# Moving one PSUM copy per pair to ScalarE, and the loads of the gate's weights and of w_out, in an attention and two-MoE kernel

## The chip, the core and the metric

The kernel runs on one core of a Trainium2 chip. A core has five engines, each with an instruction queue of its own that runs in order: TensorE (PE, matmuls, writes to PSUM only), VectorE (DVE), ScalarE (ACT), GpSimd (POOL) and SyncE (SP, which here issues nearly all DMAs). SBUF is the working memory, PSUM takes matmul results, DRAM lies behind 16 DMA engines. The metric is the device time of one execution in microseconds, lower is better.

## The reference

Three layers, on 4 batches of 448 tokens with 12 heads of 64 (1792 tokens, width 768):

```
attention:  q_n, k_n = rmsnorm(q)*g_q, rmsnorm(k)*g_k
            x = softmax(q_n @ k_n.T / sqrt(64)) @ v            # 48 (batch, head) pairs of 448 x 448
MoE 1:      h = x @ w_in            # 768 -> 2048
            g = where(h > 0, h, exp(min(h, 0)) - 1)            # ELU
            y = g @ w_out           # 2048 -> 768
MoE 2:      logits = y @ w_gate     # 768 -> 8 experts
            route tokens greedily by sorted logits, 224 per expert
            out[token] = relu(y @ w1[e]) @ w2[e]               # 768 -> 1024 -> 768
```

`w_in` and `w_out` arrive as 64-bit floats, the rest as 32-bit floats. To keep enough precision with 16-bit matmuls, most operands are split into a high and a low fp16 half, and a product is three matmuls (high x high, low x high, high x low).

## The kernel before

The first part runs attention for all batches and, one batch behind it, the hidden layer of MoE 1. The unit of attention is a *pair* of heads (`Pair`, 24 of them, numbered 0 to 23); two pairs share a `Duo`, which loads q, k and v, normalises q and k and turns them. A pair has 448 query rows, in three blocks of 128 (j = 0, 1, 2) and a tail of 64 (j = 3). For each block:

- `scores`: six matmuls for two heads A and B into two PSUM tiles `ps`, VectorE takes each row's maximum (L533), ScalarE the exponential with its row sum (L535);
- `weights`: VectorE takes reciprocals (L540, L541), GpSimd scales the rows (L545);
- `turn_p`: TensorE transposes A's weights, with a corner of B's, into the PSUM tile `ta` and B's into `tb`; ScalarE copies `ta` (128x512) to `PT` in SBUF (L559) and VectorE copies `tb` (128x384, L560).

After the tail, `values` multiplies with v into `po`, and ScalarE and VectorE evict it, split in halves, to `xT` (L578, L579). The PSUM tiles `ta`, `tb`, `po`, `pw` (gate products) and `pl` (logits) share the three buffers of one pool, `psT`.

`hidden(b)` multiplies `xT` of batch b with `w_in`: 16 blocks f of 18 matmuls each into `ph`, then ELU on ScalarE and VectorE (L682 to L688), and stores the result `gt` to DRAM (`g_d`, `gt_d`).

The second matrix of MoE 1 and the gate are joined ahead of time: the logits are g @ (w_out @ w_gate). So `gate_products` goes through `w_out` in 16 blocks of 128 rows. `load_steps` loads 64-bit numbers by SP into one of three buffers `st`, VectorE assembles 32-bit floats from their bits with three integer instructions per part (L374, L377, L378; a block has a part of 512 and one of 256 columns), ScalarE scales and casts (L380, L381), GpSimd subtracts to get the low half (L382). The block `wo` is stored to `wo_d` for later use (L610) and turned by two transposing DMAs (L614); `gate_product` multiplies the turned block with the gate's weights `wg16` and leaves 8 columns in `Wg` through one ScalarE and four VectorE instructions (L627 to L631). `load_gate` loads the gate's weights (L598) and splits them on ScalarE and VectorE (L599, L600). `w_in` is loaded by the same `load_steps`.

`logits` adds up four blocks of g against `Wg` into `acc` (L647, L649). For batches 2 and 3 that happens inside `hidden`; for batches 0 and 1 `late_logits` loads g back from DRAM (`gl`, L658, L659).

The order of the work is planned in steps t from -48 to 387: a pair has 16 steps, pair n starts its scores at step 16n and its `values` come at 16n+19. `at(t, f)` puts a function at a step, `Spread(gen, n, t0, t1)` spreads n steps of a generator evenly over t0 to t1, `hidden(b)` runs over the 96 steps that begin with 96(b+1)+5. From the order in which instructions are written a scheduler makes each engine's queue; it may put an instruction ahead of others written earlier if its inputs and its buffer are free. Two kinds of instruction are tied to the plan: the first integer instruction of each part of `w_in` or `w_out` (L374) can't come ahead of the last score maximum written before it, and a hidden block's first matmuls not ahead of scores written shortly before them.

After step 387 the hidden layer of batch 3, the second matrix of MoE 1, the routing and the experts follow. Their code isn't touched.

Of the kernel before, what the change touches and what calls it, by code (L numbers as in the profile page):

```python
# [8 lines left out]
F16 = mybir.dt.float16  # L9
# [246 lines left out]
def kernel(  # L256
# [14 lines left out]
    nc = tc.nc  # L271
    PE, ACT, DVE, POOL = nc.tensor, nc.scalar, nc.vector, nc.gpsimd

    B, H, S, D = q.shape
# [5 lines left out]
    P = 128  # L280
    NP = H // 2
    KC = DM // P
    NF = FF // P
    NF1 = F1 // P
    DH = DM // 2
    NJ = 3
    MAIN = NJ * P
    TAIL = S - MAIN
# [33 lines left out]
    def mm(o, l, r, key=None, **kw):  # L322

        i = PE_mm(o, l, r, **kw)  # L324
        if key is not None:
            if key in last_in_bank:
                tc.add_manual_dep(i.ins, last_in_bank[key].name, NOSYNC, reason="order in a bank")
            last_in_bank[key] = i.ins
        return i
# [6 lines left out]
    g_d = [dram.tile([P, NF, 2, MAIN], F16, name=f"g_d{b}") for b in range(B)]  # L336

    gt_d = [dram.tile([P, NF, 2, 2 * TAIL], F16, name=f"gt_d{b}") for b in range(B // 2)]
# [18 lines left out]
    def load_steps(hi, lo, src):  # L357

        w = src.shape[1]
        if src.dtype == F32:  # L360
            st = stg.tile([P, w], F32, tag="st", name="st")
            i = nc.sync.dma_start(st, src)
            if hold:
                tc.add_manual_dep(i.ins, hold[-1].ins.name, NOSYNC, reason="not before its turn")
            split(hi, lo, st, w)
            yield
            return

        for a in range(0, w, 512):
            n = min(512, w - a)  # L370
            st = stg.tile([P, n, 2], I32, tag="st", name="st")
            nc.sync.dma_start(st.rearrange("p n t -> p (n t)"), src[:, a:a + n].bitcast(I32))
            cv = gat.tile([P, n], I32, tag="cv", bufs=3, name="cv")
            i = DVE.tensor_scalar(cv, st[:, :, 1], 3, 0x3FFFFFF8, op0=ALU.logical_shift_left, op1=ALU.bitwise_and)  # L374
            if pace:
                tc.add_manual_dep(i.ins, pace[-1].ins.name, NOSYNC, reason="not before its turn")
            DVE.scalar_tensor_tensor(cv, st[:, :, 1], -0x40000000, cv, op0=ALU.bitwise_and, op1=ALU.bitwise_or)  # L377
            DVE.scalar_tensor_tensor(cv, st[:, :, 0], 29, cv, op0=ALU.logical_shift_right, op1=ALU.bitwise_or)  # L378
            cf = cv.bitcast(F32)
            ACT.activation(cf, cf, AF.Copy, scale=SW)  # L380
            ACT.copy(hi[:, a:a + n], cf)  # L381
            POOL.tensor_sub(lo[:, a:a + n], cf, hi[:, a:a + n])  # L382
            yield
# [13 lines left out]
    def key():  # L397
        n_key[0] += 1
        return n_key[0]
# [4 lines left out]
    gat = att_s.enter_context(tc.tile_pool(name="gat", bufs=2))  # L404
# [3 lines left out]
    psT = ps1.enter_context(tc.tile_pool(name="psT", bufs=3, space=PSUM))  # L408
# [89 lines left out]
    class Pair:  # L498
# [48 lines left out]
        def turn_p(s, j):  # L547

            p = s.P.pop(j)[0].rearrange("p u k -> p (u k)")
            ta = psT.tile([P, NJ + 1, P], F32, tag="pt", name="pta")  # L550
            for c in range(NJ):
                mm(ta[:, c, :], p[:, c * P:(c + 1) * P], id32, is_transpose=True, start=True, stop=True)
            mm(ta[:, NJ, :], p[:, MAIN:MAIN + 2 * TAIL], id32, is_transpose=True, start=True, stop=True)
            if j < NJ:
                tb = psT.tile([P, NJ + 1, P], F32, tag="pt", name="ptb")
                for c in range(NJ):
                    mm(tb[:, c, :], p[:, S + TAIL + c * P:S + TAIL + (c + 1) * P], id32, is_transpose=True, start=True, stop=True)
                cs = slice(j * P, (j + 1) * P)
                ACT.copy(s.PT[:, 0:NJ + 1, cs], ta)  # L559
                DVE.tensor_copy(s.PT[:, NJ + 1:, cs], tb[:, 0:NJ])  # L560
            else:
                ACT.copy(s.PT[:, 0:NJ, MAIN:S], ta[:, 0:NJ, 0:TAIL])
                ACT.copy(s.PT[0:TAIL, NJ, MAIN:S], ta[0:TAIL, NJ, 0:TAIL])
                DVE.tensor_copy(s.PT[:, NJ + 1:, MAIN:S], ta[:, 0:NJ, TAIL:])
                DVE.tensor_copy(s.PT[TAIL:, NJ, MAIN:S], ta[TAIL:, NJ, TAIL:])
# [31 lines left out]
    def load_gate():  # L597
        nc.sync.dma_start(wg32, w_gate.rearrange("(c p) e -> p c e", p=P))  # L598
        ACT.activation(wg16[:, :, 0:NE], wg32, AF.Copy, scale=-SW)  # L599
        DVE.scalar_tensor_tensor(wg16[:, :, NE:], wg32, -SW, wg16[:, :, 0:NE], op0=ALU.mult, op1=ALU.subtract)  # L600

    def gate_products():
        wts = None
        for f in range(NF):
            wo = gat.tile([P, 2, DM], F16, name="wo")
            yield from load_steps(wo[:, 0, :], wo[:, 1, :], w_out[f * P:(f + 1) * P, :])
            if f:
                gate_product(f - 1, wts)
                yield
            nc.sync.dma_start(wo_d[:, f], wo)  # L610
            wts = []
            for z in range(2):
                wts.append(gat.tile([P, KC, P], F16, name="wt", bufs=3))
                nc.sync.dma_start_transpose(wts[z], wo[:, z, :])  # L614
            yield
        gate_product(NF - 1, wts)
        yield

    def gate_product(f, wts):
        pw = psT.tile([P, 2 * NE], F32, tag="pt", name="pw")  # L620
        for z in range(2):
            n = NE if z else 2 * NE
            for c in range(KC):
                mm(pw[:, 0:n], wts[z][:, c, :], wg16[:, c, 0:n], start=(z == 0 and c == 0),
                   stop=(z == 1 and c == KC - 1), skip_group_check=True)
        t = gat.tile([P, NE], F32, name="wgt")
        ACT.copy(t, pw[:, NE:])  # L627
        DVE.tensor_add(t, t, pw[:, 0:NE])
        DVE.tensor_copy(Wg[:, f, 0:NE], t)
        DVE.tensor_copy(Wg[:, f, WG:], t)  # L630
        DVE.tensor_sub(Wg[:, f, NE:2 * NE], t, Wg[:, f, 0:NE])  # L631

    LG = 4

    def logits(pool, tag, b, gs):

        pl = pool.tile([P, S], F32, tag=tag, name="pl")
        kk = key()
        for i, (g, f) in enumerate(gs):
            for z, (o, n) in enumerate(((0, WG), (WG, NE))):  # L640
                mm(pl[o:o + n], Wg[:, f, o:o + n], g[:, z, :], key=kk,
                   start=(i == 0), stop=(i == len(gs) - 1), skip_group_check=True)
        n = WG + NE
        for o, w, c in ((b * MAIN, MAIN, 0), (B * MAIN + b * TAIL, TAIL, MAIN)):
            a = acc[:, o:o + w]
            if gs[0][1] == 0:
                DVE.tensor_copy(a, pl[0:n, c:c + w])  # L647
            else:
                DVE.tensor_add(a, a, pl[0:n, c:c + w])  # L649

    LB = 2

    def late_logits(b):
        for f in range(0, NF, LG):
            gs = []
            for i in range(f, f + LG):
                gl = gat.tile([P, 2, S], F16, bufs=LG, name="gl")
                nc.sync.dma_start(gl[:, :, 0:MAIN], g_d[b][:, i])  # L658
                nc.sync.dma_start(gl[:, :, MAIN:S], gt_d[b // 2][:, i, :, b % 2 * TAIL:(b % 2 + 1) * TAIL])  # L659
                gs.append((gl, i))  # L660
            yield
            logits(psT, "pt", b, gs)
            yield

    def hidden(b, xT):

# [28 lines left out]
        if b >= LB:  # L695
            logits(psT, "pt", b, gs[NF - LG:NF])
# [14 lines left out]
    def chain_gens(gens):  # L711
        for g in gens:
            yield from g

    def w_in_steps(u):
        for c in range(KC):
            load_w_in(u, c)
            yield
# [5 lines left out]
    def at(t, f, *a):  # L724
        todo.setdefault(t, []).append((f, a))

    NG = NF * (2 + DM // 512 + 1)
    spreads = [
        Spread(w_in_steps(0), KC, 40, 96),
        Spread(chain_gens(w_in_steps(i) for i in range(1, FF // WB)), KC * (FF // WB - 1), 96, 176),  # L730
        Spread(gate_products(), NG, 180, 280),
        Spread(chain_gens(late_logits(b) for b in range(LB)), 2 * LB * NF // LG, 295, 400),
    ]
    at(-47, load_gain)
    at(-30, load_gate)
    NSTEP = B * SEQ
    for b in range(B):
        xT = big.tile([P, KC, 2, S], F16, name="xT")
# [122 lines left out]
    for o in range(0, NCH, h):  # L861
        pt = psR.tile([P, h, n], F32, tag=f"rt_pb{4 if o else 0}", name="plt")
# [152 lines left out]
```

## Time and profile before

| what | value |
|---|---|
| median of three runs | 1150.81 us (1146.79 to 1153.8) |
| the profiled execution | 1149.89 us |
| its span, first to last instruction | 1148.2 us |
| mean granted TensorE clock | 0.968 of full speed |
| busy: PE, DVE, ACT, POOL | 1037.0, 787.0, 538.5, 354.1 us |

Busy time is the union of an engine's instructions; matmuls are pipelined and their ends are modelled, so a busy TensorE isn't one at its peak. An instruction that waits inside an engine for a shared resource counts as busy too. The DMA share is the mean busy share of the 16 DMA engines.

### The profile page before, as it was taken

The page shows a single profiled execution, that of the slowest core. Times are in us where ns is not written, and L with a number is a line of the kernel's source. Part 1 is how long each engine was busy: PE and PEld are TensorE (multiplying, and loading weights), DVE is VectorE, ACT ScalarE, POOL GpSimd, SP SyncE. Part 2 cuts the span into 40 slices and gives each one's busy share as a digit, 9 for nine tenths or more (in the row PEclk, how much of TensorE's full clock was granted, in tenths as well). Part 3 has the DMA queues.
Part 4 walks back from the last instruction along what each step waited for, and adds up shares of the span by engine and source line. Part 5 has one row for each costly group of instructions (what it writes and reads, how often), then busy time and mean ns, then how long its engine had stood idle before and what let it go on. Part 6 is the DMA issues. An engine that isn't in the chain of part 4 may idle for free.

```text
span 1148.2 us, 19348 instructions
## 1 busy us (share of the span) xinstructions
PE 1037.0 (90%) x7030; PEld 608.9 (53%) x7030; DVE 787.0 (69%) x1567; ACT 538.5 (47%) x1099; POOL 354.1 (31%) x462
## 2 busy tenths in 40 slices
PE   0687879897989989999999999999999799999997
PEld 0233434443544444444444545555546688888885
DVE  3798898999988775654334778887786556666620
ACT  2676677776867765554441111011112455555510
POOL 3677686657756542221001000000000412222100
PEclk9977889999999999999999999999999899999999
DMA  6355575559998736334922151131133778777710
GB/s 173 80 123 130 136 206 164 152 162 246 259 246 207 193 74 135 97 80 148 398 78 69 59 196 59 49 132 49 49 104 100 238 244 247 255 252 255 239 41 25
DMA packets 190319, 176.48 MB, mean 154 GB/s; under 512 B 114704, under 2 KB 161808, under 8 KB 189456
## 3 DMA queue, kind: packets, MB, share of 16 engines
q1 hardware_dynamic: 186064, 163.78, 49.7%
q0 software_dynamic: 3328, 11.01, 3.0%
q8 instruction: 55, 0.90, 0.3%
q10 hardware_dynamic: 832, 0.46, 0.1%
q14 instruction: 40, 0.33, 0.1%
HBM read 125.92 MB, written 31.98 MB: 138 GB/s over the span
## 4 chain that ended last, share of the span: by engine, by line
PE 51%; DVE 18%; DMA 11%; issue 10%; ACT 5%; POOL 3%; SPq 2%; POOLq 0%; DVEq 0%; ACTq 0%
PE py L324 18%; PE ph L324 11%; DMA st<-in_moe_w_dram 4%; PE pye L324 4%; PE po L324 4%; PE phe L324 3%; DVE sm L533 2%; PE ps L324 2%; PE rt_pc L324 2%; DVE cv L377 2%; PE pta L324 2%; DMA qn<-in_q_dram 2%; PE pl L324 1%; DVE cv L378 1%; DVE rt_C L127 1%
## 5 line engine op out<-in xcount | busy, mean ns | idle before, releaser
L324 PE MATMUL ph<-xT,w_in 128*128 128x448 f16 x1152 | 247.2, 359 | 7.8 <-DVE elu_g L685 4.8
L324 PE MATMUL py<-w_out,g 128*128 128x384 f16 x1152 | 203.8, 328 | 0.0
L324 PEld LDWEIGHTS <-w_in 128*128 128x128 f16 x1152 | 108.0, 99 | 125.4 <-issue 44.7
L545 POOL TENSOR_SCALAR pe<-pe,sm 128x448 f32<-128x448 f32 x168 | 127.0, 766 | 141.0 <-DVE sm L541 78.9
L351 DVE SCALAR_TENSOR_TENSOR w<-st,w 128x768 f16<-128x768 f32 (+1 forms) x112 | 119.4, 1073 | 72.1 <-ACT w L350 65.8
L324 PEld LDWEIGHTS <-g 128*128 128x128 f16 x1152 | 107.3, 98 | 81.4 <-issue 18.5
L350 ACT ACTIVATE w<-st 128x768 f16<-128x768 f32 (+1 forms) x112 | 103.8, 933 | 89.3 <-DMA st<-in_moe_w_dram 84.0
L324 PE MATMUL ps<-kT,qT 64*128 64x448 f16 (+1 forms) x576 | 94.3, 382 | 54.5 <-ACT pe L535 29.2
L535 ACT ACTIVATE pe<-ps,sm 128x448 f32<-128x448 f32 x168 | 105.7, 633 | 50.1 <-DVE sm L533 47.6
L324 PE MATMUL pye<-w,hT 128*112 128x512 f16 (+1 forms) x768 | 126.4, 326 | 0.0
L127 DVE TENSOR_SCALAR rt_C<-rt_row,rt_m 128x1792 f16<-128x1792 f32 x98 | 107.3, 1149 | 8.2 <-PE rt_pc L324 7.4
L533 DVE TENSOR_REDUCE sm<-ps 128x1 f32<-128x448 f32 x168 | 100.2, 614 | 17.8 <-PE ps L324 15.5
L324 PEld LDWEIGHTS <-w 128*128 128x128 f16 x1152 | 110.4, 99 | 3.3 <-DVE xTe L922 1.2
L324 PE MATMUL phe<-xTe,w 128*128 128x224 f16 x1080 | 109.2, 261 | 2.1 <-DVE xTe L922 1.1
L324 PEld LDWEIGHTS <-hT 128*112 128x112 f16 x768 | 91.6, 130 | 32.1
L815 ACT ACTIVATE xh<-py 128x384 f16<-128x384 f32 x28 | 13.7, 490 | 176.6 <-PE py L324 159.2
L324 PEld LDWEIGHTS <-qT 64*128 64x128 f16 (+1 forms) x576 | 27.5, 100 | 99.0 <-issue 65.9
L324 PE MATMUL pta<-id,pe 128*128 128x128 f32 x384 | 65.3, 293 | 12.7 <-POOL pe L545 4.7
L685 DVE SCALAR_TENSOR_TENSOR elu_g<-ph,elu_e 128x448 f32<-128x448 f32 x64 | 39.6, 618 | 48.0 <-ACT elu_e L683 47.7
L972 POOL DMA_INDIRECT out_dram<-yo,idx x16 | 18.5, 1155 | 173.9 <-DVE yo L971 172.3
L324 PEld LDWEIGHTS pta<-id,pe 128*128 128x128 f32 x384 | 46.1, 148 | 43.1 <-POOL pe L545 16.0
L201 POOL MEMSET rt_c<- 128x8 f16 x8 | 0.9, 123 | 210.1 <-DVE rt_c L207 206.0
(176 smaller groups left out, 1475.1 us busy)
## 6 DMA issues: line engine op xcount, KB each, us to landing
st<-in_moe_w_dram SPq DMA_DIRECT2D x48, 512.0 KB
st<-in_moe_w_dram SPq DMA_DIRECT2D x64, 384.0 KB
st<-in_moe_w_in_dram SPq DMA_DIRECT2D x24, 512.0 KB
g_d<-gt SPq DMA_DIRECT2D x64, 192.0 KB
g<-g_d SPq DMA_DIRECT2D x16, 768.0 KB
st<-in_moe_w_out_dram SPq DMA_DIRECT2D x16, 512.0 KB
gl<-g_d SPq DMA_DIRECT2D x32, 192.0 KB
wo_d<-wo SPq DMA_DIRECT2D x16, 384.0 KB
```

The source lines that it names most:

```text
L127: i = DVE.tensor_scalar(C.rearrange("p c t -> p (c t)"), row, m[:, s:s + 1], None, op0=ALU.is_le)
L324: i = PE_mm(o, l, r, **kw)
L350: ACT.activation(hi, st, AF.Copy, scale=SW)
L351: DVE.scalar_tensor_tensor(lo, st, SW, hi, op0=ALU.mult, op1=ALU.subtract)
L377: DVE.scalar_tensor_tensor(cv, st[:, :, 1], -0x40000000, cv, op0=ALU.bitwise_and, op1=ALU.bitwise_or)
L378: DVE.scalar_tensor_tensor(cv, st[:, :, 0], 29, cv, op0=ALU.logical_shift_right, op1=ALU.bitwise_or)
L533: i = DVE.tensor_reduce(out=st[:, 0, u:u + 1], in_=ps[u], axis=AX.X, op=ALU.max, negate=True)
L535: ACT.activation(p[:, u, :], ps[u], AF.Exp, bias=st[:, 0, u:u + 1], accum_out=st[:, 1, u:u + 1])
L545: POOL.tensor_scalar(p[:, u, :], p[:, u, :], st[:, 2, u:u + 1], 1.0, op0=ALU.mult, op1=ALU.mult)
L685: DVE.scalar_tensor_tensor(gf, ph, -SG / SH, e, op0=ALU.mult, op1=ALU.min)
L815: ACT.activation(xh[:, 0], py, AF.Copy, scale=-SX2 / (SG * SW))
L972: st = POOL.indirect_dma_start(out=out, out_offset=bass.IndirectOffsetOnAxis(ap=idx[:, 1, 2 * e + hh:2 * e + hh + 1], axis=0), in_=yo, in_ ...
```

## The change

Four edits:

- for the middle block of each pair (j = 1) `tb` is copied to `PT` by ScalarE, no longer by VectorE;
- `gate_products` is spread over steps 240 to 368, before over 180 to 280;
- `late_logits` takes the two batches in turn for each group of four blocks, before one batch after the other, and is spread over steps 285 to 400, before 295 to 400;
- `load_gate` is put at step 100, before at -30.

The list `ready` is only bookkeeping while the program is built: it makes sure that logits are written after the gate products that they read.

```diff
@@ Pair.turn_p
                 ACT.copy(s.PT[:, 0:NJ + 1, cs], ta)
-                DVE.tensor_copy(s.PT[:, NJ + 1:, cs], tb[:, 0:NJ])
+                (ACT.copy if j == 1 else DVE.tensor_copy)(s.PT[:, NJ + 1:, cs], tb[:, 0:NJ])
@@ gate_products
+    ready = []
+
     def gate_products():
-        wts = None
         for f in range(NF):
...
             if f:
                 gate_product(f - 1, wts)
+                ready.append(f - 1)
                 yield
...
         gate_product(NF - 1, wts)
+        ready.append(NF - 1)
         yield
@@ logits
+        assert gs[-1][1] in ready
@@ late_logits
-    def late_logits(b):
+    def late_logits():
         for f in range(0, NF, LG):
-            gs = []
-            for i in range(f, f + LG):
-                gl = gat.tile([P, 2, S], F16, bufs=LG, name="gl")
-                nc.sync.dma_start(gl[:, :, 0:MAIN], g_d[b][:, i])
-                nc.sync.dma_start(gl[:, :, MAIN:S], gt_d[b // 2][:, i, :, b % 2 * TAIL:(b % 2 + 1) * TAIL])
-                gs.append((gl, i))
-            yield
-            logits(psT, "pt", b, gs)
-            yield
+            for b in range(LB):
+                gs = []
+                for i in range(f, f + LG):
+                    gl = gat.tile([P, 2, S], F16, bufs=LG, name="gl")
+                    nc.sync.dma_start(gl[:, :, 0:MAIN], g_d[b][:, i])
+                    nc.sync.dma_start(gl[:, :, MAIN:S], gt_d[b // 2][:, i, :, b % 2 * TAIL:(b % 2 + 1) * TAIL])
+                    gs.append((gl, i))
+                yield
+                logits(psT, "pt", b, gs)
+                yield
@@ the plan
-        Spread(gate_products(), NG, 180, 280),
-        Spread(chain_gens(late_logits(b) for b in range(LB)), 2 * LB * NF // LG, 295, 400),
+        Spread(gate_products(), NG, 240, 368),
+        Spread(late_logits(), 2 * LB * NF // LG, 285, 400),
...
-    at(-30, load_gate)
+    at(100, load_gate)
```

## Rows read from the trace of the kernel before

**Rows 1.** The page: busy us (share of the span) xinstructions, and the chain.

```profile
PE 1037.0 (90%) x7030; PEld 608.9 (53%) x7030; DVE 787.0 (69%) x1567; ACT 538.5 (47%) x1099; POOL 354.1 (31%) x462
...
PE 51%; DVE 18%; DMA 11%; issue 10%; ACT 5%; POOL 3%; SPq 2%; POOLq 0%; DVEq 0%; ACTq 0%
```

**Rows 2.** Timeline of ScalarE: start us, us, engine, line, operation, out<-in.

```profile
254.67 0.53 ACT L578 ACTIVATE xT<-po 128x448 f16<-128x448 f32 x1
```

**Rows 3.** Stretches: from:to, us, busy us (x) of each engine, clock, DMA share, GB/s.

```profile
core 0: us, PE busy (x) PEld busy (x) DVE busy (x) ACT busy (x) POOL busy (x), PEclk, DMA share, GB/s
55.71:254.67 198.96, 171.53 (x893) 78.93 (x894) 178.63 (x341) 143.47 (x333) 136.35 (x164) 0.89 0.58 149
169.28:190.06 20.78, 20.78 (x124) 10.55 (x124) 16.46 (x30) 14.83 (x35) 11.86 (x14) 1.00 0.56 153
235.89:254.67 18.78, 18.78 (x108) 8.65 (x107) 16.29 (x39) 15.17 (x38) 8.46 (x12) 1.00 0.55 155
254.67:280.48 25.81, 21.77 (x145) 10.59 (x144) 25.70 (x55) 18.01 (x45) 19.96 (x24) 1.00 1.03 251
280.48:303.92 23.44, 18.61 (x130) 10.12 (x130) 22.78 (x58) 16.05 (x42) 16.50 (x16) 0.85 0.99 253
303.92:330.27 26.35, 24.46 (x156) 12.00 (x156) 25.73 (x59) 21.72 (x55) 17.65 (x24) 1.00 0.97 247
...
407.19:421.56 14.37, 10.10 (x71) 5.26 (x71) 12.50 (x30) 9.37 (x28) 8.41 (x13) 1.00 0.08 17
254.67:359.69 105.02, 92.10 (x601) 45.64 (x600) 99.32 (x229) 75.12 (x185) 69.57 (x82) 0.95 0.99 251
359.69:521.06 161.37, 151.66 (x970) 74.89 (x969) 107.97 (x269) 99.61 (x245) 59.86 (x87) 1.00 0.51 120
521.06:538.59 17.53, 17.53 (x106) 8.99 (x108) 8.15 (x19) 8.33 (x19) 2.21 (x4) 1.00 0.36 90
```

**Rows 4.** Stretches, instructions on `ph` alone: us, then PE, DVE, ACT busy.

```profile
169.28:190.06 20.78, 12.53 (x60) 1.23 (x2) 1.09 (x2) 1.00 0.56 153
235.89:254.67 18.78, 9.31 (x42) 1.24 (x2) 1.62 (x3) 1.00 0.55 155
...
407.19:421.56 14.37, 1.46 (x6) 0.00 (x0) 0.00 (x0) 1.00 0.08 17
```

**Rows 5.** A stretch, instructions on `cv` alone: us, then DVE, ACT, POOL busy.

```profile
218.00:410.00 192.00, 58.59 (x104) 35.37 (x70) 38.40 (x37) 0.96 0.82 208
```

**Rows 6.** A stretch, instructions on `wgt` alone: us, then DVE, ACT busy.

```profile
254.67:420.00 165.33, 18.10 (x64) 2.57 (x16) 0.97 0.86 214
```

**Rows 7.** Timeline of VectorE: one unit of logits, of nine up to 521 us.

```profile
461.14 0.66 DVE L649 TENSOR_TENSOR acc<-acc,pl 40x384 f32<-40x384 f32 x2
```

**Rows 8.** Groups by line and shape: xcount | busy us, mean ns | idle before.

```profile
L559 ACT COPY PT<-pta 128x512 f32<-128x512 f32 x72 | 41.8, 583 | 9.7 <-PE pta L324 9.5
...
L560 DVE COPY PT<-ptb 128x384 f32<-128x384 f32 x72 | 39.4, 547 | 4.8 <-PE ptb L324 4.7
...
L377 DVE SCALAR_TENSOR_TENSOR cv<-st,cv 128x512 int32<-128x512 int32 x40 | 36.7, 916 | 0.0
...
L562 ACT COPY PT<-pta 128x192 f32<-128x192 f32 x24 | 7.6, 318 | 5.0 <-PE pta L324 5.0
```

**Rows 9.** Line L377: duration ns min/median/max, first and last start us, forms.

```profile
L377 DVE SCALAR_TENSOR_TENSOR cv<-st,cv x56: 411/681/2171, 66.6 to 389.1; 128x512 int32<-128x512 int32 x40, 128x256 int32<-128x256 int32 x16
```

**Rows 10.** Timeline of the first microseconds: SP, ScalarE and VectorE around the gate's weights.

```profile
11.36 1.54 SPq L372 DMA_DIRECT2D st<-in_moe_w_in_dram  x3
...
11.77 0.24 ACT L599 ACTIVATE wg<-wg 128x48 f16<-128x48 f32 x1 [3.03 <-DMA wg<-in_moe_w_gate_dram]
...
11.92 0.95 ACT L451 ACTIVATE sq<-kn 128x896 f32<-128x896 f32 x1
12.04 1.99 DVE L600 SCALAR_TENSOR_TENSOR wg<-wg,wg 128x48 f16<-128x48 f32 x1 [0.38 <-ACT wg L599]
13.96 1.07 DVE L452 TENSOR_REDUCE ss<-sq 128x14 f32<-128x896 f32 x1
```

## The prediction

> **What bounds the kernel now.** I read the busy shares and the chain of waits first, then the span cut into stretches at the ends of the attention pairs, then the groups by line, then the first 30 us. Over the whole span TensorE is busy 90% and VectorE 69%, and the chain is half TensorE and a fifth VectorE [rows 1]; a mean over stages with different limits, so the stretches decide. A pair (two heads, 16 steps of the planner) ends when its values are evicted to `xT`, at step 16n+19: pair 10's eviction starts at 254.67 us [rows 2]. The starts of these evictions are the cuts of the stretches.
>
> Pairs 11 to 13 (steps 180 to 227) are where `w_out` is split now. VectorE is busy 25.70 of 25.81, 22.78 of 23.44 and 25.73 of 26.35 us there, together 74.2 of 75.6: it is the bound. Pairs 15 to 22 take 161.4 us, VectorE only 108.0 of it, TensorE 151.7: there TensorE is the bound, and VectorE has 53 us to spare. Pairs 1 to 10 are mixed: VectorE 178.6 of 199.0 us, TensorE 171.5 [rows 3]. After step 387 the kernel runs on what attention has left behind; the change touches nothing there, so what the end of pair 23 gains or loses is carried to the end.
>
> **The change, part by part.** The sum is made against the profiled execution, 1149.89 us (span 1148.2 and 1.7 around it); the median of the three runs shown is 1150.81, 0.9 us more.
>
> *Stretch 1, pairs 11 to 14, 105.0 us before.* `w_out` goes from steps 180–280 to 240–368, so its loads, bit splits, casts, stores, transposes and gate products leave these four pairs, except for the last four steps. What is late next is TensorE: without `w_out`, pairs 7 and 10 took 20.78 and 18.78 us with TensorE busy throughout [rows 3], and ran 60 and 42 matmuls of the hidden layer in them [rows 4]. The plan gives 48 per pair, a third of the way from 42 to 60, so 19.4 us a pair, 77.6 for four: **27.4 us less**. Ends: 14.4 a pair, as pair 17 without hidden matmuls, would be 47 less; 22.2, the mean of pairs 7 to 9 (169.28 to 235.89 us), 16 less.
>
> *Stretch 2, pairs 15 to 22, 161.4 us before.* The splits: 104 instructions on `cv` cost VectorE 58.59 us between 218 and 410 us (96 are `w_out`'s, six per block of 128 rows), so 3.38 per block [rows 5]; four small gate instructions per block, 18.10/16 = 1.13 [rows 6]. A block costs 4.51 us. Before, 100 steps held 16 blocks, 2.56 per pair; now 128 steps hold them, 2.0 per pair. Pairs 11 to 13 cost VectorE 24.74 each; 0.56 blocks less is 22.21. Nine logits units that fall here add 0.66 us each [rows 7], 0.74 per pair. The copy that goes to ScalarE takes off 0.547 [rows 8]. That is 22.41 us of VectorE per pair, with the idle share of pairs 11 to 13 (75.6/74.2) 22.83, and 182.6 for eight: **21.3 us more**. So the work doesn't vanish in the slack: eight pairs at 20.2 had 13.5 us of VectorE each, and 9 us of `w_out` lifts them past TensorE's need. Ends: if TensorE stays the bound, 5 us more (its share of the gate products); if the pairs run as pairs 11 to 14 did, 26.3 each, 48.7 more.
>
> How much of a block's price is blocking: the 512-wide L377 takes 916 ns in the mean while the median over both widths is 681 and the longest 2171 [rows 8, 9]. The Trainium skill (SBUF — State Buffer, Who interferes with whom) says that a VectorE instruction with two SBUF inputs fully blocks against a GpSimd instruction that reads SBUF. The trace agrees: GpSimd is busy 69.6 of 105.0 us in stretch 1 but 59.9 of 161.4 in stretch 2 [rows 3]. By that rule the excess could go where GpSimd rests: an estimate of 0.33 us per block, 5 us in all, 1133 instead of the sum below; but a block brings its own GpSimd subtractions along, so I leave it out.
>
> DMA: the busy share is 0.99 over 105.0 us and 0.51 over 161.4 [rows 3], 104 and 82 us. With 0.55 left over 77.6, 143 us remain for 182.6, a share of 0.79; two loads, one store and two transposes per block pass through SP's queue between q and k loads with more room than before. I cost this at nothing; the last rival prices its loss.
>
> *Pair 23.* In the VectorE-bound stretch TensorE fills its gaps with hidden matmuls ahead of the plan, as it did before: pair 17 had 6 left, and took 14.4 us [rows 3, 4]. That now comes at the end, and pair 23 goes from 17.53 to about 14.4: **3.1 us less**. Ends: 0 and 3.1.
>
> *The copy in pairs 1 to 10.* Ten instructions of 547 ns leave VectorE, 5.5 us. ScalarE copies 512 columns in 583 ns and 192 in 318 [rows 8], so 384 in about 0.48; it is busy 143 of 199 us and its queue is in order, so exponentials wait behind it. VectorE is the bound for perhaps half of this stretch: **2.2 us less**; ends 5.5 less and 2.4 more (half of ten ScalarE copies on the path). In pairs 0, 11 to 14 and 23 it is worth nothing while TensorE or the first loads are late; if that cover is gone it is worth another 3 us. In stretch 2 it is already in the sum.
>
> *The gate's weights.* `load_gate` goes from step -30 to 100. Now ScalarE waits 3.03 us for this load at 11.77 us, then squares k; VectorE's split of it (1.99 us) holds the sum of k's squares until 13.96 [rows 10]. The square of k also waits for `gain` (they share a buffer) and takes 0.95 us, so it can't end before about 12.7; only the split's delay goes, 13.96 less 12.7, 1.3 us. But nothing holds the load back except its place in SP's queue, so it can be issued right behind the three `w_in` loads that start at 11.36 us and take 1.54 to issue, and ScalarE may then wait for it ahead of k's halves. I take **0**, between 1.3 less and 2.4 more; the row nearest to it is the same wait, 3.03 us.
> The Trainium skill (DMA: Bandwidth & Descriptors, Queues, rings and completion order) has each DMA engine consume one ring's descriptors in order, so the load would land after those 1.5 MB; no row shows it behind them. By that rule the 2.4 us end would hold and the sum would be 1141.
>
> *Late logits* keep 16 units, start at 285 instead of 295 and take both batches per group of blocks. Each waits for gate products planned at least 11 steps earlier and its own loads; 0, with the last rival for the loss of that lead.
>
> Sum: 1149.9 - 27.4 + 21.3 - 3.1 - 2.2 + 0 = **1138.5 us**.
>
> **The rivals.**
> - *TensorE bounds both stretches* (stretch 2 costs 5 more, not 21.3): 1122. For it: VectorE's 53 us of slack. Against: 16 blocks x 4.51 = 72 us don't fit in 53.
> - *Stretch 1 doesn't shrink to TensorE's pace*: at 22.2 a pair it saves 16.2, and the rest cancels: 1149.7. For it: pairs 7 to 9 ran so. Against: these carried `w_in`'s splits, which are done by then.
> - *Stretch 2 stalls in order*: turned blocks, values, gate products and logits now all go through the three PSUM buffers of `psT`, and TensorE's queue is in order, so each late eviction by VectorE stops hidden matmuls too. Before, gate products and logits never met. At 26.3 a pair (what pairs 11 to 14 took) this adds 48.7 instead of 21.3: 1166. It decides from 24.3 us a pair on, where stretch 2 eats all that the rest saves. Against: longer time per block (11.4 us instead of about 10).
> - *The splits don't move*: if they ran early after all, only the copy would be left, 2.2 us and at most 3.3 more in pairs 11 to 16: 1145; but each split is tied to a score reduction of its own step, so I give it next to nothing and count it with the second rival.
>
> **How the numbers follow.** Forecast 0.47 (own range 1129 to 1147), TensorE in both 0.12, cancelling 0.19, stalls 0.22. Faster by over 0.5% (below 1144.1; half a per cent is about what a measurement of this kernel can tell from no change): 0.42 + 0.12 + 0.02 = 0.56. Within: 0.05 + 0.15 + 0.02 = 0.22. Slower: 0.02 + 0.20 = 0.22. The range 1123 to 1162 leaves out about half of each outer rival.
>
> **What would show it.** Right: pairs 11 to 14 near 78 us with TensorE full; pairs 15 to 22 near 183 with VectorE over 95% busy; pair 23 short; 48 copies of L560 on VectorE. Wrong: pairs 15 to 22 above 194 us or with VectorE under 85%; TensorE waiting for `pw`, `pl` or their DMAs; k's halves waiting for the gate's weights. The forecast falls if stretch 1 saves under 16 us.

## The result, and the profile after

The changed kernel takes 1135.59 us in the median of four runs (1133.87 to 1135.79), the kernel before 1151.24 (1146.79 to 1153.8) beside it: a ratio of 0.9865, with an interval of 0.9833 to 0.9897. The forecast was 1138.5. A later repeat (e9) gave 0.9891 (0.9859 to 0.9923). So the change takes 9 to 19 us away (the two intervals together, 0.8 to 1.7%). The ratios here and below are taken over all runs of both kernels and can differ by 0.001 from the quotient of the two medians.

The profiled execution took 1135.53 us. The page's busy shares and its chain:

```profile
PE 1034.7 (91%) x7030; PEld 607.8 (54%) x7030; DVE 776.1 (68%) x1543; ACT 547.8 (48%) x1123; POOL 360.8 (32%) x462
...
PE 58%; DVE 13%; issue 9%; DMA 9%; ACT 5%; POOL 3%; SPq 1%; POOLq 0%; DVEq 0%; ACTq 0%
```

TensorE's share of the chain rises from 51 to 58%, VectorE's falls from 18 to 13 [rows 1]. The same stretches as in [rows 3], cut again at the starts of the evictions to `xT` (pair 10 at 246.92 us, pair 14 at 323.41, pair 22 at 512.08, pair 23 at 527.55):

```profile
53.55:246.92 193.37, 166.30 (x881) 77.08 (x882) 169.60 (x323) 143.40 (x337) 139.05 (x163) 0.91 0.58 150
...
323.41:345.72 22.31, 20.52 (x119) 9.11 (x118) 20.89 (x47) 17.22 (x44) 15.62 (x20) 0.85 0.94 228
345.72:370.19 24.47, 24.47 (x163) 12.08 (x163) 23.13 (x56) 20.24 (x51) 14.78 (x18) 1.00 0.84 218
370.19:399.56 29.37, 24.08 (x155) 11.26 (x154) 25.55 (x53) 18.20 (x46) 18.55 (x23) 0.88 0.75 170
...
419.49:440.49 21.00, 17.93 (x118) 8.79 (x116) 12.57 (x37) 11.53 (x29) 7.50 (x13) 0.92 0.97 239
440.49:465.65 25.16, 25.16 (x166) 12.37 (x167) 19.73 (x50) 18.02 (x44) 9.89 (x14) 1.00 0.90 236
...
246.92:323.41 76.49, 75.51 (x442) 36.92 (x443) 55.34 (x114) 54.88 (x129) 39.71 (x52) 1.00 0.45 110
323.41:512.08 188.67, 177.94 (x1173) 86.70 (x1172) 156.39 (x389) 131.65 (x328) 95.55 (x120) 0.95 0.83 203
512.08:527.55 15.47, 14.42 (x87) 7.83 (x89) 4.16 (x9) 4.88 (x10) 0.00 (x0) 1.00 0.32 80
```

Stretch 1 (pairs 11 to 14) falls from 105.0 to 76.5 us with TensorE full, stretch 2 (pairs 15 to 22) rises from 161.4 to 188.7, pair 23 falls from 17.5 to 15.5. In stretch 2 VectorE is busy 156.4 of 188.7 us, 83%, and TensorE 177.9, 94%: pair 20 is full on TensorE, pair 15 nearly full on VectorE, pairs 17 and 19 on neither. Pairs 1 to 10 are 5.6 us shorter.

Where the hidden layer's matmuls ran, before and after (instructions on `ph` alone; us, then PE, DVE, ACT busy). The kernel before:

```profile
254.67:359.69 105.02, 48.08 (x222) 7.34 (x12) 5.93 (x11) 0.95 0.99 251
359.69:521.06 161.37, 72.84 (x343) 12.37 (x20) 10.90 (x20) 1.00 0.51 120
```

The changed kernel:

```profile
246.92:323.41 76.49, 39.71 (x183) 6.17 (x10) 5.50 (x10) 1.00 0.45 110
323.41:512.08 188.67, 90.57 (x405) 13.53 (x22) 11.90 (x22) 0.95 0.83 203
```

Stretch 1 lost 39 of these matmuls and stretch 2 gained 62: besides the 39, 8 that pair 23 had done (46 before, 38 after) and 15 that had run after pair 23. Before, TensorE had filled its gaps in stretch 1 with hidden matmuls ahead of the plan; with `w_out` gone there are no gaps and nothing runs ahead, so stretch 2 has to do them. Its busy time rises by 26.3 us (151.7 to 177.9), nearly all of the 27.3 us that the stretch grew; 17.7 of it is on `ph`. Not all of the rise is additional work: the granted clock of the stretch was 1.00 before and is 0.95 here. In e9, the same kernel again, the same 1173 matmuls were busy 3.6 us less at 0.97:

```profile
322.82:508.20 185.38, 174.29 (x1173) 85.25 (x1172) 156.13 (x389) 131.46 (x327) 95.60 (x120) 0.97 0.84 207
```

### The profile page after: what moved, and what is told of

Read it like the earlier page. It is cut to its first block, busy times and chain, and to the rows that moved or that the text cites. A ratio compares the mean times of both kernels' runs of the same rounds, so it can differ in the third digit from the quotient of the medians.

```text
span 1133.0 us, 19335 instructions
## 1 busy us (share of the span) xinstructions
PE 1034.7 (91%) x7030; PEld 607.8 (54%) x7030; DVE 776.1 (68%) x1543; ACT 547.8 (48%) x1123; POOL 360.8 (32%) x462
## 4 chain that ended last, share of the span: by engine, by line
PE 58%; DVE 13%; issue 9%; DMA 9%; ACT 5%; POOL 3%; SPq 1%; POOLq 0%; DVEq 0%; ACTq 0%
PE py L324 18%; PE ph L324 15%; PE po L324 5%; PE pye L324 4%; DMA st<-in_moe_w_dram 4%; PE ps L324 4%; PE phe L324 3%; PE pta L324 3%; PE rt_pc L324 2%; DVE sm L533 2%; PE ptb L324 1%; DMA qn<-in_q_dram 1%; DVE rt_C L127 1%; PE pl L324 1%; DVE w L351 1%
## 5 line engine op out<-in xcount | busy, mean ns | idle before, releaser
L324 PEld LDWEIGHTS <-w_in 128*128 128x128 f16 x1152 | 106.2, 99 | 118.0 <-issue 39.0
L545 POOL TENSOR_SCALAR pe<-pe,sm 128x448 f32<-128x448 f32 x168 | 131.8, 794 | 114.2 <-DVE sm L541 64.5
L324 PEld LDWEIGHTS <-qT 64*128 64x128 f16 (+1 forms) x576 | 27.4, 101 | 100.4 <-issue 69.1
L324 PEld LDWEIGHTS pta<-id,pe 128*128 128x128 f32 x384 | 46.4, 148 | 49.1 <-POOL pe L545 23.6
```

The costliest lines, as they stand in the source:

```text
L545: POOL.tensor_scalar(p[:, u, :], p[:, u, :], st[:, 2, u:u + 1], 1.0, op0=ALU.mult, op1=ALU.mult)
```

## Experiments

The runs e1 to e4 were made on one chip, e5 to e8 on a second and e9 to e12 on a third; the kernel before took 1156.06, 1154.46 and 1151.5 us there. The expectations reckon their totals from 1149.9, so the gains have to be compared and not the totals.

The first table adds up what the profiles say, in us, from the starts of the evictions. "Middle" is pairs 11 to 23; its TensorE idle time is the stretch less the busy time. One profile per run, so a few us are the spread of single executions. "Copy" and "gate" say whether tb's middle copy is on ScalarE and the gate's weights at step 100.

| kernel | w_out | copy | gate | pair 0 ends | pairs 1–10 | 11–14 | 15–22 | 23 | middle | TensorE idle in it |
|---|---|---|---|---|---|---|---|---|---|---|
| before | 180–280 | no | no | 55.7 | 199.0 | 105.0 | 161.4 | 17.5 | 283.9 | 22.6 |
| e1 | 180–280 | yes | no | 55.4 | 196.1 | 111.1 | 162.9 | 19.2 | 293.2 | 24.0 |
| e3 | 180–280 | no | yes | 54.1 | 200.6 | 106.2 | 163.6 | 17.5 | 287.3 | 23.2 |
| e4 | 240–368 | no | no | 56.3 | 199.2 | 75.9 | 190.5 | 14.2 | 280.5 | 14.9 |
| e2 | 240–368 | no | yes | 54.1 | 197.4 | 75.9 | 185.8 | 14.2 | 275.8 | 10.8 |
| changed | 240–368 | yes | yes | 53.6 | 193.4 | 76.5 | 188.7 | 15.5 | 280.6 | 12.8 |
| e9, changed again | 240–368 | yes | yes | 54.5 | 191.9 | 76.5 | 185.4 | 15.5 | 277.3 | 13.1 |

Two theories were set against each other. Theory V is the prediction's: VectorE bounds the stretches in which `w_out`'s bits are split. Theory P came from the profile after: the middle takes TensorE's work, which no edit changes, plus TensorE's idle time.

**One edit at a time.** e4 keeps only `w_out`'s steps and the late logits:

```diff
-        Spread(gate_products(), NG, 180, 280),
-        Spread(chain_gens(late_logits(b) for b in range(LB)), 2 * LB * NF // LG, 295, 400),
+        Spread(gate_products(), NG, 240, 368),
+        Spread(late_logits(), 2 * LB * NF // LG, 285, 400),
```

> The kernel before with w_out's steps at 240 to 368 and the late logits in turn from 285, nothing else. Theory V: stretch 1 27 us less, stretch 2 25 us more with VectorE over 95% busy, pair 23 3 us less: about 1145. Theory P (time from step 179 to 387 is TensorE's work plus its idle time, hidden matmuls that ran ahead in stretch 1 go to stretch 2): 281 us for these 13 pairs as in the changed kernel, VectorE 80 to 90% busy in stretch 2, total 1145 to 1148.

Measured: 1144.28 us against 1156.06 on the same chip, 0.9907 (0.9883 to 0.9932). This is the part that pays, 8 to 14 us, more than either theory's total gives from 1149.9 (2 to 5). `w_out`'s steps and the late logits were not tried apart. Its stretches:

```profile
255.52:331.37 75.85, 75.40 (x438) 37.08 (x438) 56.49 (x114) 52.65 (x122) 39.45 (x51) 1.00 0.43 106
331.37:521.89 190.52, 177.28 (x1178) 85.67 (x1177) 160.09 (x399) 129.59 (x323) 93.12 (x120) 0.98 0.83 202
```

VectorE is busy 84% of stretch 2, not over 95%, as theory P had it. The three kernels with `w_out` early have a mean middle of 288.1 us with 23.3 idle on TensorE, the four with it late 278.6 with 12.9: the 9.6 us that are gained are 10.4 of TensorE's idle time, and its busy time stays at 265 to 266 in the mean. Single profiles scatter more, from 261.3 to 269.1 us of busy time, so the means carry this and no two rows do: from the kernel before to the changed one the middle fell by 3.3 us only.

e1 keeps only the copy:

```diff
-                DVE.tensor_copy(s.PT[:, NJ + 1:, cs], tb[:, 0:NJ])
+                (ACT.copy if j == 1 else DVE.tensor_copy)(s.PT[:, NJ + 1:, cs], tb[:, 0:NJ])
```

> The kernel before with one edit: the middle block's tb copied by ScalarE. Theory V (VectorE bounds the stretches in which the bit splits run, so 0.55 us less per pair counts in pairs 1 to 16): 2 to 9 us less, 1142 to 1149, with pairs 1 to 10 about 5 us shorter as in the changed kernel. Theory P (the gain of the changed kernel in pairs 1 to 10 comes from another order of the queues, not from the copy): within 2 us of the kernel before.

Measured: 1155.14 against 1156.06, 0.9995 (0.9975 to 1.0016): nothing. The pieces of its one profile aren't zero:

```profile
55.42:251.55 196.13, 167.44 (x897) 77.41 (x897) 171.98 (x332) 145.85 (x342) 138.76 (x162) 0.91 0.58 150
251.55:362.68 111.13, 98.77 (x607) 46.73 (x606) 99.93 (x225) 78.70 (x190) 70.56 (x83) 0.91 0.99 236
```

Pairs 1 to 10 gain 2.8 us, and stretch 1 takes 6.1 more in this profile: there VectorE's busy time is the same as before (99.9 against 99.3) though four copies are gone, and TensorE's is 6.7 us more, at a granted clock of 0.91 against 0.95. Of theory V's 2 to 9 us the interval leaves only the lowest end, 2.9 at most.

e2 is the changed kernel without the copy (that line put back).

> The changed kernel with its copy put back on VectorE: only w_out, late logits and the gate's weights are moved. Theory V: the sum of the prediction without the copy, 1149.9 - 27.4 + 21.3 + 4.5 - 3.1 = about 1145. Theory P (w_out's move nets 3 us, startup 2, the rest comes later): 1141 to 1147; if the copy does nothing, 1136 as the changed kernel.

Measured: 1141.03 against 1156.06, 0.988 (0.986 to 0.990). That lies between the two measurements of the changed kernel (0.9865 and 0.9891), so what the copy is worth in the total stays open; it is under about half a per cent either way. Theory V's sum without the copy, 5 us less than the kernel before, falls short of the 12 to 16 that the interval gives. In pairs 1 to 10 it shows: the five profiles without it have 197.4 to 200.6 us there (before, e2, e3, e4, e11), the nine with it 191.0 to 196.1 (e8, with all three copies on ScalarE, among them).

e3 moves only the load of the gate's weights:

```diff
-    at(-30, load_gate)
+    at(100, load_gate)
```

> The kernel before with one edit: the load of the gate's weights at step 100. The first scores start 1.5 us earlier, as in the changed kernel. If a shift of the start is carried to the end: 1.5 to 2 us less, about 1149. If TensorE's full stretches absorb it: no change. If the new order of the queues matters more than the shift: anything within 5 us either way.

Measured: 1154.73 against 1156.06, 0.9994 (0.9973 to 1.0016). Pair 0 ends 1.6 us earlier and pairs 1 to 10 take 1.7 more; the total shows nothing, and the interval is too wide to tell a shift of 1.5 us from none.

**Which engine bounds stretch 2.** Three kernels add or take work on one engine, with everything else as in the changed kernel. e5 does the third integer instruction of each part of `w_out` twice, which leaves the same bits:

```diff
-            DVE.scalar_tensor_tensor(cv, st[:, :, 0], 29, cv, op0=ALU.logical_shift_right, op1=ALU.bitwise_or)
+            for _ in range(2 if w == DM else 1):
+                DVE.scalar_tensor_tensor(cv, st[:, :, 0], 29, cv, op0=ALU.logical_shift_right, op1=ALU.bitwise_or)
```

> The changed kernel with the third integer instruction of each part of w_out done twice on VectorE (it leaves the same bits): 32 instructions, 0.68 us for 512 columns and 0.41 for 256, 17 us more VectorE work in steps 240 to 368 (more where blocked). Theory V (VectorE bounds stretch 2): 12 to 17 us longer, about 1150. Theory P (TensorE bounds it, VectorE has 32 us of idle time there): 0 to 6 us longer, 1136 to 1142.

e10 leaves that instruction out:

```diff
-            DVE.scalar_tensor_tensor(cv, st[:, :, 0], 29, cv, op0=ALU.logical_shift_right, op1=ALU.bitwise_or)
+            if w != DM:
+                DVE.scalar_tensor_tensor(cv, st[:, :, 0], 29, cv, op0=ALU.logical_shift_right, op1=ALU.bitwise_or)
```

> The changed kernel without the third integer instruction on w_out's parts (the three lowest bits of each weight's mantissa are left out): about 17 us less VectorE work in steps 240 to 368, TensorE's work as it is. Theory V (VectorE bounds stretch 2): 12 to 17 us less than the changed kernel. Theory P (TensorE bounds it, and VectorE decides only in part of it, 40% by the run with these instructions doubled): 3 to 8 us less, stretch 2 about 182 us.

e6 does each gate product's matmuls twice:

```diff
-        for z in range(2):
+        for z in (0, 1, 0, 1):
```

> The changed kernel with the gate product's matmuls of each w_out block done twice (the second pass starts the sum anew): 192 matmuls more on TensorE, about 9 us of its busy time in steps 240 to 368, nothing more on VectorE. Theory V: 0 to 3 us longer. Theory P: 6 to 9 us longer, about 1143.

Measured: e5 1145.35 against 1154.46, 0.9916 (0.9884 to 0.9948); e6 1145.24 against 1154.46, 0.993 (0.9903 to 0.9958); e10 1132.34 against 1151.5, 0.9823 (0.9789 to 0.9858), with the changed kernel at 1139.45 on e10's chip. What each edit did to its engine, as instructions on `cv` (DVE, ACT, POOL busy) or `pw` (PE, DVE, ACT busy), the stretches running from the start of pair 13 to the end of 23. The changed kernel, `cv` alone:

```profile
281.43:527.55 246.12, 54.24 (x96) 32.55 (x64) 32.42 (x32) 0.96 0.74 182
```

The changed kernel, `pw` alone:

```profile
281.43:527.55 246.12, 7.50 (x192) 2.47 (x16) 2.74 (x16) 0.96 0.74 182
```

e5, `cv` alone, and then its middle with the columns of [rows 3]:

```profile
284.12:536.58 252.46, 74.01 (x128) 32.67 (x64) 33.91 (x32) 0.96 0.73 177
```

```profile
249.54:536.58 287.04, 270.49 (x1699) 132.50 (x1701) 227.91 (x543) 191.22 (x464) 138.68 (x172) 0.96 0.69 167
```

e10 likewise:

```profile
282.23:519.89 237.66, 33.57 (x64) 33.22 (x64) 34.12 (x32) 0.99 0.77 188
```

```profile
247.75:519.89 272.14, 262.19 (x1699) 129.59 (x1701) 197.69 (x479) 189.95 (x464) 132.11 (x172) 0.99 0.73 176
```

e6, `pw` alone, and its middle:

```profile
280.44:531.00 250.56, 12.48 (x384) 2.51 (x16) 2.68 (x16) 0.97 0.73 179
```

```profile
245.92:531.00 285.08, 271.78 (x1888) 134.24 (x1890) 213.76 (x511) 190.91 (x465) 133.42 (x172) 0.98 0.69 168
```

The middles of the changed kernel itself, here and in e9:

```profile
246.92:527.55 280.63, 267.87 (x1699) 131.46 (x1701) 215.89 (x511) 191.40 (x464) 135.26 (x172) 0.96 0.69 171
```

```profile
246.37:523.68 277.31, 264.21 (x1699) 130.01 (x1701) 215.59 (x511) 191.16 (x464) 135.30 (x172) 0.98 0.71 173
```

Against 279.0 us, the mean of these two: 19.8 us more of splits on VectorE cost 8.1, 20.7 us less gave 6.8 back, and 5.0 us more on TensorE cost 6.1. So VectorE's splits count for a third to two fifths of their size, TensorE's work for about all of it; but the two profiles of one kernel differ by 3.3 us, so these shares are rough. (In e5 VectorE's whole busy time rose by 12.2 us only, of which 8.1 is two thirds.) I had put the doubled matmuls at 9 us; they are busy only 5.0 more, and they also hold their `psT` buffer longer, which isn't separated here. The timed runs show the direction for e10 (7.1 us less on one chip); e6 (0.993) and e5 (0.9916) lie above the changed kernel's 0.9865 and 0.9891, but the intervals overlap with the second. Theory V's 12 to 17 us are in neither profile, though e5's 8.1 is above theory P's 0 to 6 too: TensorE bounds most of stretch 2, with VectorE late now and then.

**What VectorE's lateness costs.** Theory P takes TensorE's work as fixed and its idle time as all that can change. The rows above say that this is half of it: the same 1699 matmuls were busy 270.5 us in e5 at a granted clock of 0.96 and 262.2 in e10 at 0.99. Against the mean of the changed kernel, TensorE's own busy time makes 4.5 of e5's 8.1 us and 3.9 of e10's 6.8, idle time the rest. Pair 19 of the changed kernel shows how the two go together (timeline: start us, us, engine, line, operation, out<-in, the wait before it):

```profile
424.70 0.29 DVE L374 TENSOR_SCALAR cv<-st 128x256 int32<-128x256 int32 x1 [1.92 <-DMA st<-in_moe_w_out_dram]
...
425.37 0.16 DVE L541 RECIPROCAL sm<-sm 128x2 f32<-128x2 f32 x1
...
425.72 1.30 POOL L545 TENSOR_SCALAR pe<-pe,sm 128x448 f32<-128x448 f32 x2 [2.39 <-DVE sm L541]
...
427.04 0.72 PE L324 MATMUL pta<-id,pe 128*128 128x128 f32 x4 [3.07 <-POOL pe L545]
```

VectorE's queue stands 1.92 us at a split whose load of `w_out` hasn't landed; the reciprocal of the softmax, the scaling on GpSimd and the transposes on TensorE come behind it. TensorE is idle for 3 us and then runs at a mean clock of 0.57, most of it at 1.2 of 2.4 GHz, until 431 us (stretches with the columns of [rows 3]):

```profile
424.00:427.00 3.00, 0.00 (x0) 0.00 (x0) 1.21 (x5) 1.00 (x3) 1.28 (x2) 1.00 1.02 306
427.00:431.00 4.00, 3.96 (x15) 2.28 (x16) 2.25 (x7) 2.76 (x7) 1.30 (x4) 0.57 1.28 248
431.00:440.49 9.49, 9.49 (x66) 3.85 (x65) 6.14 (x19) 4.95 (x12) 1.17 (x3) 1.00 0.85 211
```

In pair 17 another thing makes VectorE late: an instruction on two columns (L540, median 0.16 us over pairs 13 to 23) takes 1.87 us beside a GpSimd multiplication, and TensorE waits 2.88 us for the reciprocal behind it. The granted clock of that pair is 0.88:

```profile
380.76 2.08 POOL L454 TENSOR_TENSOR qn<-qn,gain 128x896 f32<-128x896 f32 x1
...
381.00 1.87 DVE L540 TENSOR_SCALAR sm<-sm 128x2 f32<-128x2 f32 x1
...
384.48 1.08 PE L324 MATMUL pta<-id,pe 128*128 128x128 f32 x4 [2.88 <-DVE sm L541]
```

These are single places of one profile; no run changes the loads or GpSimd's work alone.

**Thinner still.** e7, and e12 with the same kernel on the chip of e9, spread `w_out` over steps 180 to 368; e11 does that with `tb` copied by VectorE:

```diff
-        Spread(gate_products(), NG, 240, 368),
+        Spread(gate_products(), NG, 180, 368),
```

> The changed kernel with w_out's steps over 180 to 368 instead of 240 to 368: 1.36 blocks per pair instead of 2.0. Theory V: VectorE needs 22.4 - 0.64*4.5 = 19.5 us a pair, below TensorE, so stretch 1 at about 20 and stretch 2 at about 20.5 a pair: 8 to 15 us less than the changed kernel, 1121 to 1128. Theory P: TensorE's work is the same, only its 10.7 us idle time in stretch 2 can go: 0 to 8 us less, 1128 to 1136.

> The changed kernel once more, on the same chip as the next three, so that these can be set against it. Both theories: 0.983 to 0.990 of the kernel before.

> The changed kernel with w_out's steps over 180 to 368, on the same chip as the changed kernel. Theory V: 8 to 15 us less than the changed kernel. Theory P, and the first run of it: 0 to 6 us less.

> w_out's steps over 180 to 368 and tb copied by VectorE as before. Theory V: the copy is worth 0.55 us a pair where VectorE is late, so 3 to 8 us more than with the copy on ScalarE. Theory P: TensorE bounds most of it, 0 to 4 us more.

Measured: e7 1135.59 against 1154.46, 0.9827 (0.9793 to 0.986). On one chip: the changed kernel (e9) 1139.45, 0.9891 (0.9859 to 0.9923); e12 1136.9, 0.9873 (0.9838 to 0.9908); e11 1139.77, 0.9889 (0.9855 to 0.9922). The middle of e12:

```profile
249.22:328.76 79.54, 75.63 (x478) 36.98 (x477) 68.62 (x155) 59.94 (x146) 51.28 (x66) 1.00 0.86 204
328.76:514.91 186.15, 179.27 (x1160) 87.58 (x1161) 134.97 (x342) 124.90 (x307) 78.42 (x109) 0.98 0.68 165
514.91:524.71 9.80, 8.57 (x55) 4.65 (x57) 2.91 (x7) 3.10 (x7) 0.00 (x0) 1.00 0.39 94
```

```profile
249.22:524.71 275.49, 263.46 (x1691) 129.21 (x1691) 206.49 (x504) 187.94 (x460) 129.69 (x175) 0.99 0.72 174
```

Theory V wanted 8 to 15 us less than the changed kernel. There are 2.6 on the same chip, inside the intervals, and 12.0 us of TensorE's idle time remain. VectorE in stretch 2 is down to 73% and the DMA share to 0.68 (0.83 in the changed kernel), and the stretch takes as long, which speaks against either as its main bound. So this is at best a slight gain over the changed kernel, not shown. e11 against e12 is the copy alone on one chip: 2.9 us, inside the intervals too, in theory P's range and just under theory V's. The middles are equal (275.3 and 275.5 us); pairs 1 to 10 differ by 3.4.

**More of the copy.** e8 gives all three blocks' `tb` to ScalarE:

```diff
-                (ACT.copy if j == 1 else DVE.tensor_copy)(s.PT[:, NJ + 1:, cs], tb[:, 0:NJ])
+                (ACT.copy if j >= 0 else DVE.tensor_copy)(s.PT[:, NJ + 1:, cs], tb[:, 0:NJ])
```

> The changed kernel with all three blocks' tb copied by ScalarE, none by VectorE: 1.1 us a pair more off VectorE, 0.97 more on ScalarE. Theory V: another 3 to 12 us less, 1124 to 1133. Rival: ScalarE, in order and already 70% busy in pairs 1 to 16, becomes the late one, its exponentials wait behind the copies: 2 to 8 us more, 1138 to 1144.

Measured: 1143.03 against 1154.46, 0.9903 (0.9874 to 0.9933). Theory V's gain isn't there; the centre is worse than the changed kernel's, with intervals that overlap. Its stretch 2:

```profile
325.31:520.40 195.09, 181.54 (x1190) 86.98 (x1189) 145.13 (x375) 138.85 (x347) 95.44 (x121) 0.95 0.83 198
```

VectorE is 11 us lighter there than in the changed kernel and the stretch 6 us longer (10 against e9). That ScalarE's order is the reason, as its rival had it, was not tried apart.

## Why the prediction was right, and where it was not

The total came out near the forecast (1138.5 against 1135.59), and half of the mechanism. That the total fits is in part luck. In the two profiles everything up to the end of pair 23 sums to 11.0 us less, where the terms gave 11.4; but stretch 2 cost 6.0 us more than forecast, and pairs 0 to 10 gained about 5.5 more (5.6 against 2.2 for the copy, 2.2 against 0 for the start). The profile's other 4.1 us fell after pair 23, where nothing was forecast.

- *Stretch 1, 27.4 us less*: 28.5 in the profile (105.0 to 76.5), with TensorE busy 75.5 of 76.5 us. Right, by its own reason; e2, e4 and e9 have 75.9 to 76.5 too.
- *Stretch 2, 21.3 us more*: 27.3. The size was near, the reason failed. The step said that VectorE's 22.83 us a pair bound it and that VectorE would be over 95% busy; by the mark set there, under 85% means wrong, and it was 83%. Two terms were off. The rest of VectorE's work per pair, without `w_out`, was taken as 24.74 - 2.56 x 4.51 = 13.2 from pairs 11 to 13, 13.4 with the logits added and the copy taken off; measured, (156.4 - 49.0 for `cv` - 14.0 for the gate) / 8 is 11.7. And TensorE's need was taken from the same pairs of the kernel before, in which 343 hidden matmuls ran; after, 405 run. The prediction used this running ahead for pair 23 and forgot it here. It also had no term for the clock, which fell from 1.00 to 0.95 in this stretch. By theory P both stretches together are the sum, and there the two errors met: the middle fell by 9.6 us in the means of the table, where the terms gave 27.4 - 21.3 + 3.1 = 9.2.
- *A block's price of 4.51 us of VectorE*: (54.24 + 13.98)/16 = 4.26, from the row of the changed kernel for `cv` above and this one of the same stretch for `wgt` (DVE, ACT busy):

```profile
281.43:527.55 246.12, 13.98 (x64) 2.74 (x16) 0.96 0.74 182
```

  The splits kept their price, 3.38 us a block before and 3.39 after; the four gate instructions fell from 1.13 to 0.87, the first cast of `wgt` from 500 to 232 ns. The part that the Trainium skill would lay to blocking (SBUF — State Buffer, Who interferes with whom) hardly moved: over 512 columns of `w_out` L377 took 778 ns in the mean before (the 14 from 254.67 us on) and 739 after, L378 711 and 738. So the 5 us of that estimate weren't there, and VectorE wasn't the main bound anyway. The 916 ns that the estimate started from is a mean over 40 instructions, 24 of which split `w_in`.
- *Pair 23, 3.1 us less*: 2.1.
- *The copy in pairs 1 to 10, 2.2 us less*: 5.7 in the means (the seven profiles of kernels with the middle copy, `w_out` planned up to step 368 and the late gate load have 191.0 to 195.1 us, the five without the copy 197.4 to 200.6), the far end of the range. On its own price the guess was near:

```profile
L559 ACT COPY PT<-pta 128x512 f32<-128x512 f32 x72 | 42.1, 584 | 9.6 <-PE pta L324 9.2
...
L560 DVE COPY PT<-ptb 128x384 f32<-128x384 f32 x48 | 26.4, 549 | 8.6 <-PE ptb L324 8.5
...
L560 ACT COPY PT<-ptb 128x384 f32<-128x384 f32 x24 | 11.7, 486 | 0.2 <-PE ptb L324 0.2
```

  ScalarE takes 486 ns, VectorE 549. In the total the gain is lost again in later pairs (e1) or can't be told from the spread (e2, e11).
- *The gate's weights, 0*: pair 0 ends at 54.6 us in the mean of the eleven kernels with the late load and at 55.8 in that of the three with the early one, 1.2 us, near the better end. The first microseconds of the changed kernel show why:

```profile
10.00 0.95 ACT L451 ACTIVATE sq<-kn 128x896 f32<-128x896 f32 x1 [1.15 <-DVE ss L452]
...
11.55 1.08 DVE L452 TENSOR_REDUCE ss<-sq 128x14 f32<-128x896 f32 x1
...
12.89 0.38 SPq L598 DMA_DIRECT2D wg<-in_moe_w_gate_dram  x1
...
19.05 0.24 ACT L599 ACTIVATE wg<-wg 128x48 f16<-128x48 f32 x1
...
20.18 0.20 DVE L600 SCALAR_TENSOR_TENSOR wg<-wg,wg 128x48 f16<-128x48 f32 x1
```

  The load is indeed issued right behind the three `w_in` loads, but the scheduler put ScalarE's instruction behind both halves of k and q, where it waits for nothing. The square of k ran at 10.00 us, before `gain`: that it waits for `gain` was wrong. The sum of its squares does, as it stands behind the making of `gain` (L315, at 11.41 us after 1.45 us of waiting for its load) in VectorE's queue. The Trainium skill's rule (DMA: Bandwidth & Descriptors, Queues, rings and completion order) isn't contradicted: in e5 this load, issued at 13.38 us behind the three of `w_in`, releases ScalarE only at 20.09, 6.7 us later; in the kernel before, issued at 7.70 ahead of them, it did so at 11.77, 4.1 us later. ScalarE waited just 0.24 us for it in e5, as it had work until then. VectorE's split takes 0.20 us here, 1.99 before, when GpSimd worked beside it.
- *The rivals.* "TensorE in both" named the bound rightly and its time (1122) wrongly, as it gave stretch 2 no more hidden matmuls to do. The stall in order did not come to 26.3 us a pair (23.6 in the mean), but single pairs stall so: pair 17 takes 29.4. TensorE waits there for the softmax's weights, behind a late VectorE, and not for `pw` or `pl`. The cancelling rival fails with stretch 1.

What stays open: the copy's worth in the total, what the late loads and GpSimd's multiplications cost over the whole stretch, and the late logits apart from `w_out`. After pair 23 the profiled execution gained another 4.1 us (609.6 to 605.5); the other profiles have 606 to 612 whatever the edit, so this is spread.

## What to carry to other kernels

When work moves between stretches of an in-order pipeline with a filler (here the hidden layer's matmuls), add up the bottleneck engine's work over all stretches that the filler can reach; what can be gained is that engine's idle time, and what it loses in clock behind such idle time; the stretch that gets the work also gets back what had run ahead. Here a helper engine at 83% beside a bound one at 94% still charged something like a third to two fifths of every microsecond that it got. Taking half a microsecond per pair off the helper was worth nothing that could be measured by itself, and moving all three copies to the other engine brought no more than moving one.

## What the runs showed of the hardware that was not expected

- A VectorE instruction of two SBUF inputs over 48 columns took 1.99 us beside a GpSimd multiplication and 0.20 us alone; one with a single input over two columns (L540) took 1.87 us beside one, where its median is 0.16.
- After 3.07 us without a matmul TensorE's granted clock stood at half for most of the next 4 us, although TensorE was busy 3.96 of these 4.
- The same 192 additional gate matmuls added 5.0 us to TensorE's busy time, 26 ns each, while one is recorded at 166 to 170 ns: so narrow matmuls in a row overlap, and a group's mean times its count says little about what it costs.
